# Writing the product of gate and value back into PSUM and splitting it from there, in a windowed attention with two gated MLPs

## The chip, the cores and the metric

The kernel runs on one core of a Trainium2 chip. The metric is the device time of one execution in microseconds, the median of several runs. The engines are named as in the profile: PE (TensorE matmuls) and PEld (its weight loads), DVE (VectorE), ACT (ScalarE), POOL (GpSimd) and SP (the queue that issues all DMAs). SBUF is the working memory of all engines; PSUM is the memory into which PE writes its products.

## The reference, cut to what matters

```python
scores = np.where(mask, scale * q @ k.T, -1e9)        # 4 x 8 heads, 576 positions, window 64
x = (softmax(scores) @ v)                             # -> 2304 tokens x 512
gate = 1.0 / (1.0 + np.exp(-(x @ w_gate)))            # 512 x 1536
x = (gate * (x @ w_val)) @ w_out                      # first MLP ("phase 0")
return ((x @ w_a) * (x @ w_b)) @ w_out2               # second MLP ("phase 1")
```

The six weight matrices come as 64-bit numbers and are decoded on the chip. Every matmul is done three times over, with both operands split into a high part of PE's reduced float format and the low rest (high by high, high by low, low by high).

## The kernel before, in words

The 2304 tokens stand in nine blocks of 256 columns. A slice of 128 of the 1536 hidden features is called F; each F has three weight tiles, `a` (gate), `b` (value) and `o` (out). For each slice the kernel makes a gate product and a value product on PE, multiplies the two, splits the result into high and low part, and later projects it with `o`.

The work runs through four stages. A **ramp** (0 to 75 us) has the attention and the first hidden slices in an order written out by hand. The **first MLP of the front blocks** (75 to 340 us) runs with the rest of the attention beside it. Then comes the **second MLP of the front blocks** (340 to about 612 us), while the weights of that MLP are still being decoded. Last come **the back blocks** (612 us to the end), whose weights are read back in split form. Outside the ramp and some runs of instructions that `in_order` ties, the order on each engine comes from the framework's scheduler, which has its own simulated times.

There are two ways in which gate times value is made.

- `hidden` calls `up` twice and then `gated`. `up` fills two PSUM tiles, `gps` (gate) and `vps` (value), of the pool `ps_gv`, which has three banks. `gated` moves the gate to SBUF as `hr` (ACT, a tanh in phase 0, a copy in phase 1), DVE multiplies `hr` with `vps` into `hr`, and `split_hidden` makes the two parts: ACT writes the high part `hh` from `hr`, then DVE writes the low part `hl` from `hr` and `hh`.
- `quad` takes two slices of tokens and features at once with seven products in place of eight (a Strassen-like scheme), in the order 1, 5, 6, 2, 7, 4, 3, each of six 512-column matmuls, into three banks `qa`, `qb`, `qc` of `ps_gv` and `ps_at` in turn, so that quad n+2 uses the pool of quad n. Between products ACT copies `qa` to SBUF (`keep_sum`: tiles `r`, line L845) and DVE adds `r` to a bank (`plus`, L848). `finish(0, ..)` and `finish(1, ..)` make the two results: gate `g[i]` times value (L853 in phase 0, L857 in phase 1) into `g[i]`, then the split as above, `hh`/`hl` for the first result and one tile `h` with both parts for the second.

In the quads of phase 0 but the last (`second is None`), the back blocks go on with seven products in the projection too: there `difference` (L900) reads `g[0]` and `g[1]` in SBUF, and the second result is not split.

A bank of a pool goes to the next tile in the program whose turn it is when its last reader in the program's order has come; the bank that is let go first is given out first.

The weight decode of one tile runs over three engines in a row: ACT `low` (L375) and `ex` (L378), DVE `wi` (L381, L384), POOL `wi` (L388), DVE `ex` (L394), ACT the high part (L400), DVE or POOL the low part (L403). For the quads POOL and ACT then make four sums of `a` and `b` (`s` L447, `wq` L449 and L450).

Of the kernel before, what the change touches and what calls it, by code (L numbers as in the profile page):

```python
# [14 lines left out]
AF = mybir.ActivationFunctionType  # L15
ALU = mybir.AluOpType
# [5 lines left out]
def tile_window_attention_gated_mlps(ctx, tc, q, k, v, w1g, w1v, w1o, w2a, w2b, w2o, out):  # L22
    nc = tc.nc
# [54 lines left out]
    for e in range(2):  # L78
        rows = slice(e * WIN, (e + 1) * WIN)
        nc.gpsimd.affine_select(  # L80
            out=mask_n[rows], in_=mask_n[rows], pattern=[[1, P]], compare_op=ALU.is_ge,
# [3 lines left out]
            out=mask_n[rows], in_=mask_n[rows], pattern=[[-1, P]], compare_op=ALU.is_ge,  # L85
# [175 lines left out]
    def quarter(i, j, nm):  # L261
        return xs.tile([P, 2, W], F32R, tag=f"q{i}{j}", name=f"{nm}{i}{j}")
# [32 lines left out]
    def whole(steps):  # L295
        while True:
            try:
                next(steps)
            except StopIteration as end:
                return end.value  # L300
# [172 lines left out]
    def split_hidden(phase, dst, hr):  # L473

        factor = 0.5 if phase == 0 else 1.0
        hh, hl = dst
        nc.scalar.activation(out=hh, in_=hr, func=AF.Copy, scale=factor)  # L477
        yield
        nc.vector.scalar_tensor_tensor(
            out=hl, in0=hr, scalar=factor, in1=hh.bitcast(F32), op0=ALU.mult, op1=ALU.subtract  # L480
        )
        yield dst

    def gated(phase, ps, n):
        hr = tmp.tile([P, W], F32, tag="hr", name="hr")[:, 0:n]
        if phase == 0:

            nc.scalar.activation(out=hr, in_=ps["a"], func=AF.Tanh, scale=0.5)
            yield
            nc.vector.scalar_tensor_tensor(out=hr, in0=hr, scalar=1.0, in1=ps["b"], op0=ALU.add, op1=ALU.mult)  # L490
        else:
            nc.scalar.activation(out=hr, in_=ps["a"], func=AF.Copy)
            yield
            nc.vector.tensor_tensor(out=hr, in0=ps["b"], in1=hr, op=ALU.mult)
        yield
        h = tuple(hp.tile([P, W], F32R, tag=f"h{p}", name=f"h{p}")[:, 0:n] for p in "hl")
        yield from split_hidden(phase, h, hr)

    def up(ps, nm, w, x):
        ps[nm] = ps_gv.tile([P, x[0].shape[-1]], F32, tag="gv", name="gps" if nm == "a" else "vps")  # L500
# [2 lines left out]
    def hidden(phase, w, x):  # L503
        ps = {}
        for nm in "ab":
            up(ps, nm, w, x)
        *_, h = gated(phase, ps, x[0].shape[-1])
        return h
# [312 lines left out]
    def multiply(ps, w, x, first):  # L821
        (wh, wl), (xh, xl) = w, x
        n = 0
        for c in range(2):
            for a, b in ((wh, xh), (wh, xl), (wl, xh)):
                nc.tensor.matmul(  # L826
                    ps, lhsT=a[:, c * P:(c + 1) * P], rhs=b[:, c, :], start=first and n == 0, stop=n == 5,
                    skip_group_check=True,
                )
                n += 1  # L830
# [3 lines left out]
    def products(ph, w, x, g, second):  # L834


        nquad[0] += 1
        bank, tag = (ps_gv, "gv") if nquad[0] % 2 else (ps_at, "at")
        pa, pb, pc = (bank.tile([P, W], F32, tag=tag, name=f"q{nm}") for nm in "abc")
        prod = lambda n, ps, first: multiply(ps, w[n], x[n], first)  # L840
        r, h = {}, []

        def keep_sum(ps, n):
            r[n] = late["rs"].tile([P, W], F32, tag="r", name=f"r{n}")
            nc.scalar.activation(out=r[n], in_=ps, func=AF.Copy)  # L845

        def plus(dst, ps, n):
            nc.vector.tensor_tensor(out=dst, in0=ps, in1=r[n], op=ALU.add)  # L848

        def finish(i, vv):  # L850
            if ph == 0:
                nc.scalar.activation(out=g[i], in_=g[i], func=AF.Tanh, scale=0.5)
                nc.vector.scalar_tensor_tensor(  # L853
                    out=g[i], in0=g[i], scalar=1.0, in1=vv, op0=ALU.add, op1=ALU.mult
                )
            else:
                nc.vector.tensor_tensor(out=g[i], in0=vv, in1=g[i], op=ALU.mult)  # L857
            if i == 0:
                t = tuple(hp.tile([P, W], F32R, tag=f"h{p}", name=f"h{p}") for p in "hl")
            elif second is None:  # L860
                h.append(None)
                return
            else:
                t = second()
                t = (t[:, 0], t[:, 1])
            whole(split_hidden(ph, t, g[i]))
            h.append(t)

        steps = {
            1: (lambda: prod(1, pa, True), lambda: keep_sum(pa, 1)),  # L870
            5: (lambda: prod(5, pb, True),),
            6: (lambda: prod(6, pa, False), lambda: keep_sum(pa, 2)),
            2: (lambda: prod(2, pc, True), lambda: plus(g[0], pc, 1)),
            7: (lambda: prod(7, pa, False), lambda: keep_sum(pa, 3), lambda: plus(r[3], pb, 3)),
            4: (lambda: prod(4, pa, False), lambda: finish(0, pa)),
            3: (lambda: prod(3, pb, False), lambda: plus(g[1], pb, 2)),
        }

        def step(n):
            for f in steps[n]:  # L880
                f()

        def end():
            finish(1, r[3])
            return tuple(h)

        return step, end

    def quad(ph, w, x, fill, g, second, between):
        step, end = products(ph, w, x, g, second)  # L890
        for i, n in enumerate((1, 5, 6, 2, 7, 4, 3)):
            step(n)
            fill(i)
        between()
        return end()
# [81 lines left out]
    def ramp_turns():  # L977
        waiting = []
        for n, (group, fcs) in enumerate(plan[:len(FIRST)]):
            hs = []  # L980
            for i, fc in enumerate(fcs):
                ps = {}

                def after(ps=ps, fc=fc, n=len(group) * N, hs=hs):
                    for h in gated(0, ps, n):
                        if h:
                            hs.append((parts[fc], h))
                        yield

                for nm in "ab":  # L990
                    matmuls.append(lambda ps=ps, nm=nm, fc=fc, group=group: up(ps, nm, parts[fc], x[0, group]))
                rest_of.append(after())
                for _ in range(-(-len(waiting) // (len(fcs) - i))):
                    job, number = waiting.pop(0)
                    for j in range(number):
                        cell = []

                        def mm(job=job, cell=cell):
                            m, a = next(job)
                            cell.append(a)  # L1000
                            m()

                        def ev(cell=cell):
                            cell[0]()
                            yield

                        matmuls.append(mm)
                        rest_of.append(ev())
# [104 lines left out]
    for fc in range(NF):  # L1113
# [16 lines left out]
        g = [tmp.tile([P, W], F32, tag="hr", name=f"g{i}") for i in range(2)]  # L1130
# [53 lines left out]
    for n, (ph, fc) in enumerate(steps):  # L1184
# [12 lines left out]
        if by_seven and fc % PAIR == 0:  # L1197
            g = quarter(0, 1, "g").bitcast(F32)
            g = [g[:, i] for i in range(2)]
            second = None  # L1200
        else:
            g = [tmp.tile([P, W], F32, tag="hr", name=f"g{i}") for i in range(2)]
            second = None if by_seven else (lambda a=((pairs_done - SEVEN) % 2, (fc + 1) % 2): quarter(*a, "h"))
# [4 lines left out]
        if ph and p == 0:  # L1208
            both.append((w["o"], *products(ph, w, x_ops, g, second)))
            if fc == 0:  # L1210
                continue
            since = len(nc.cur_bb.bb.instructions)
            for i, k in TOGETHER:
                both[i][1](k)
                if (i, k) == (0, 3):
                    hs.append((both[0][0], both[0][2]()))
            hs.append((w["o"], both[1][2]()))
            in_order(since, (mybir.EngineType.PE,))
        else:
            hs.append((w["o"], quad(ph, w, x_ops, slots(number, (ph, fc) == (0, PAIR)), g, second, between)))  # L1220
# [10 lines left out]
        if by_seven:  # L1231
            sums = []
            for i in range(2):
                t = late["sums"].tile([P, 2, 2, CH], F32R, tag="t", name=f"s{i}")
# [7 lines left out]
            b = {1: b11, 2: b21, 3: b22, 5: t1[0], 6: t2, 7: t3}  # L1242
# [59 lines left out]
```

## Time and profile before

| | us |
|---|---|
| median of 3 runs | 979.86 (979.34 to 980.27) |
| the profiled execution's own time | 978.29 |
| its span, first to last instruction | 976.3 |
| PE busy | 933.9 (96%) |
| DVE busy | 715.4 (73%) |
| ACT busy | 480.2 (49%) |
| POOL busy | 371.3 (38%) |

The span is what the views of the trace cover; the other 2 us of the profiled execution lie around it. An engine's busy time says how full it is, and what it waited for is read from the views of waits.

### The profile page before, as it was taken

The numbers are of one execution on the slowest core, as the hardware profiler recorded it, in microseconds if no ns is written. First come the engines' busy times: TensorE is split into PE (matmuls) and PEld (weight loads), VectorE is DVE, ScalarE is ACT, GpSimd is POOL, SyncE is SP. The second block draws the span as 40 slices with busy tenths as digits, with TensorE's granted clock in tenths as the row PEclk, the third lists the DMA queues.
The fourth block names the chain that finished last, engine by engine and source line by source line (L and its number), as shares of the span: only waits on it lengthen the run. The fifth ranks groups of instructions, "written<-read, shape, count | busy, mean of one in ns | idle before, by whom it ended". The sixth has DMA issues, their size and how long they took to land.

```text
span 976.3 us, 15657 instructions
## 1 busy us (share of the span) xinstructions
PE 933.9 (96%) x5504; PEld 775.3 (79%) x5504; DVE 715.4 (73%) x1339; ACT 480.2 (49%) x1053; POOL 371.3 (38%) x357
## 2 busy tenths in 40 slices
PE   7899999999999988989999997999999999999998
PEld 6798888887788876867777785787888888888886
DVE  6997877888754698888988976768888673444545
ACT  7896665576554455664545433563444233212111
POOL 4443233245522667785647736544440000000000
PEclk9999999999999998999999999999999999999999
DMA  9986699998852455665646567344456656554322
GB/s 221 256 217 195 245 325 323 301 309 269 260 189 87 158 177 181 228 232 200 237 162 217 210 207 244 112 153 141 151 171 217 227 191 208 161 165 114 121 65 87
DMA packets 146846, 193.70 MB, mean 198 GB/s; under 512 B 63824, under 2 KB 99152, under 8 KB 146768
## 3 DMA queue, kind: packets, MB, share of 16 engines
q1 hardware_dynamic: 146768, 192.71, 60.8%
q8 instruction: 43, 0.70, 0.3%
q14 instruction: 35, 0.29, 0.1%
HBM read 118.75 MB, written 69.47 MB: 193 GB/s over the span
## 4 chain that ended last, share of the span: by engine, by line
PE 64%; DVE 14%; POOL 10%; DMA 5%; issue 4%; ACT 2%; SPq 0%; POOLq 0%; DVEq 0%; ACTq 0%
PE qa L826 15%; PE accq L961 9%; PE qb L826 7%; PE vps L468 7%; PE gps L468 7%; PE accm L569 5%; POOL s L447 4%; PE qc L826 3%; POOL wi L388 3%; PE accy L924 3%; POOL wq L450 2%; PE accx L924 2%; DVE ex L394 2%; PE xps L228 2%; DVE wi L384 1%
## 5 line engine op out<-in xcount | busy, mean ns | idle before, releaser
L388 POOL TENSOR_TENSOR wi<-wi,low 128x512 int32<-128x512 int32 x72 | 105.8, 1469 | 137.2 <-DVE wi L384 102.9
L826 PE MATMUL qa<-op,wq 128*128 128x512 f32 x432 | 114.5, 395 | 5.7 <-ACT r L845 5.6
L826 PE MATMUL qb<-op,wq 128*128 128x512 f32 x432 | 112.2, 393 | 1.6 <-ACT op L730 0.8
L450 POOL TENSOR_TENSOR wq<-s,wq 128x256 fp32r<-128x256 f32 x96 | 90.2, 948 | 55.7 <-ACT wq L449 55.5
L845 ACT ACTIVATE r<-qa 128x512 f32<-128x512 f32 x108 | 62.0, 592 | 93.8 <-PE qa L826 78.6
L468 PE MATMUL gps<-xh,wa 128*128 128x256 f32 (+1 forms) x392 | 104.9, 336 | 0.6 <-DVE hr L490 0.6
L468 PE MATMUL vps<-xh,wb 128*128 128x256 f32 (+1 forms) x392 | 105.2, 338 | 0.0
L826 PEld LDWEIGHTS qa<-op,wq 128*128 128x128 f32 x432 | 81.7, 190 | 24.4 <-ACT r L845 7.4
L826 PEld LDWEIGHTS qb<-op,wq 128*128 128x128 f32 x432 | 81.8, 190 | 19.8 <-ACT op L730 1.0
L569 PE MATMUL accm<-hh,wo 128*128 128x512 f32 (+1 forms) x296 | 86.1, 360 | 2.8 <-DVE gacc L546 2.8
L468 PEld LDWEIGHTS gps<-xh,wa 128*128 128x128 f32 x392 | 69.2, 190 | 9.2 <-DVE hr L490 1.0
L961 PE MATMUL accq<-wo,h 128*128 128x512 f32 (+1 forms) x300 | 72.0, 383 | 4.7 <-DVE resf L965 3.1
L394 DVE SCALAR_TENSOR_TENSOR ex<-ex,wi 128x512 f32<-128x512 f32 x72 | 56.9, 790 | 25.0 <-POOL wi L388 16.2
L468 PEld LDWEIGHTS vps<-xh,wb 128*128 128x128 f32 x392 | 68.9, 190 | 7.9 <-DVE g L857 0.2
L961 PEld LDWEIGHTS accq<-wo,h 128*128 128x128 f32 x300 | 54.5, 188 | 17.7 <-DVE resf L965 4.4
L468 PE MATMUL gps<-xl,wa 128*128 128x256 f32 (+1 forms) x196 | 65.5, 334 | 0.6 <-DVE xl L237 0.6
L468 PE MATMUL vps<-xl,wb 128*128 128x256 f32 (+1 forms) x196 | 65.5, 334 | 0.0
L826 PE MATMUL qa<-op,wb 128*128 128x512 f32 x216 | 58.7, 408 | 6.0 <-ACT r L845 6.0
L477 ACT ACTIVATE hh<-g 128x512 fp32r<-128x512 f32 x36 | 22.7, 630 | 81.4 <-DVE g L857 50.8
L569 PEld LDWEIGHTS accm<-hh,wo 128*128 128x128 f32 x296 | 53.0, 191 | 11.1 <-ACT wq L449 3.2
L449 ACT ACTIVATE wq<-s 128x256 fp32r<-128x256 f32 x96 | 39.4, 414 | 41.0 <-POOL s L447 31.8
L189 ACT ACTIVATE pr<-pr,stat 128x128 f32<-128x128 f32 x144 | 54.1, 390 | 10.6 <-DVE stat L183 7.9
(173 smaller groups left out, 2152.0 us busy)
## 6 DMA issues: line engine op xcount, KB each, us to landing
wo<-ko SPq DMA_DIRECT2D x27, 512.0 KB, 4.0
wa<-ka SPq DMA_DIRECT2D x27, 512.0 KB, 4.3
st_o<-in_moe_w_out_dram SPq DMA_DIRECT2D x24, 512.0 KB, 4.7
ka<-wa SPq DMA_DIRECT2D x24, 512.0 KB, 5.0
kb<-wb SPq DMA_DIRECT2D x24, 512.0 KB, 3.9
ko<-wo SPq DMA_DIRECT2D x24, 512.0 KB, 4.2
kq<-wq SPq DMA_DIRECT2D x48, 256.0 KB, 3.3
wq<-kq SPq DMA_DIRECT2D x48, 256.0 KB, 3.1
```

The costliest lines, as they stand in the source:

```text
L189: nc.scalar.activation(out=pr[e][:, j, :], in_=pr[e][:, j, :], func=AF.Exp, bias=nmax[:, e, j:j + 1], scale=-1.0, accum_out=None if t in O ...
L388: nc.gpsimd.tensor_tensor(out=wi, in0=wi, in1=low, op=ALU.add)
L394: nc.vector.scalar_tensor_tensor(out=wf, in0=wf, scalar=SMALLEST, in1=wi.bitcast(F32), op0=ALU.is_ge, op1=ALU.mult)
L447: nc.gpsimd.tensor_tensor(out=s, in0=x, in1=y, op=op)
L449: nc.scalar.activation(out=t[:, 0], in_=s, func=AF.Copy)
L450: nc.gpsimd.tensor_tensor(out=t[:, 1], in0=s, in1=t[:, 0].bitcast(F32), op=ALU.subtract)
L468: nc.tensor.matmul(ps, lhsT=a[:, c * P:(c + 1) * P], rhs=b[:, c, :], start=(n == 0), stop=(n == 3 * NP - 1))
L569: nc.tensor.matmul(ps[:, m], lhsT=a[:, sl], rhs=b, start=k == 0, stop=k == total - 1)
L826: nc.tensor.matmul(ps, lhsT=a[:, c * P:(c + 1) * P], rhs=b[:, c, :], start=first and n == 0, stop=n == 5, skip_group_check=True,)
L845: nc.scalar.activation(out=r[n], in_=ps, func=AF.Copy)
L924: nc.tensor.matmul(bank[k], lhsT=a[n][i][:, sl], rhs=b[n][j], start=start and m == 0, stop=m == 2, skip_group_check=True,)
L961: nc.tensor.matmul(ps, lhsT=a, rhs=b, start=n == 0, stop=n == len(pairs) - 1)
```

## The change: what it does

In `gated` the product of gate and value is written over the value in its PSUM bank `vps` and no longer to `hr`; both parts are split from there. In `finish` the first result is written over `qa` and split from `qa`. The second result, where it is split, is written over `qc`: the seventh product's sum `plus(.., pb, 3)` now goes to the bank `qc` and not to the SBUF tile `r[3]`, and the product and the split read `qc`. Where `difference` later needs `g[0]` in SBUF, a new ACT copy (line 869 of the changed kernel) moves `qa` there after the split.

```diff
 def gated(phase, ps, n):
...
-            nc.vector.scalar_tensor_tensor(out=hr, in0=hr, scalar=1.0, in1=ps["b"], op0=ALU.add, op1=ALU.mult)
+            nc.vector.scalar_tensor_tensor(out=ps["b"], in0=hr, scalar=1.0, in1=ps["b"], op0=ALU.add, op1=ALU.mult)
...
-            nc.vector.tensor_tensor(out=hr, in0=ps["b"], in1=hr, op=ALU.mult)
+            nc.vector.tensor_tensor(out=ps["b"], in0=ps["b"], in1=hr, op=ALU.mult)
...
-        yield from split_hidden(phase, h, hr)
+        yield from split_hidden(phase, h, ps["b"])
...
         def finish(i, vv):
+            f = vv if i == 0 or second is not None else g[i]
             if ph == 0:
                 nc.scalar.activation(out=g[i], in_=g[i], func=AF.Tanh, scale=0.5)
                 nc.vector.scalar_tensor_tensor(
-                    out=g[i], in0=g[i], scalar=1.0, in1=vv, op0=ALU.add, op1=ALU.mult
+                    out=f, in0=g[i], scalar=1.0, in1=vv, op0=ALU.add, op1=ALU.mult
                 )
             else:
-                nc.vector.tensor_tensor(out=g[i], in0=vv, in1=g[i], op=ALU.mult)
+                nc.vector.tensor_tensor(out=f, in0=vv, in1=g[i], op=ALU.mult)
...
-            whole(split_hidden(ph, t, g[i]))
+            whole(split_hidden(ph, t, f))
+            if second is None:
+                nc.scalar.activation(out=g[i], in_=f, func=AF.Copy)
             h.append(t)
...
-            7: (lambda: prod(7, pa, False), lambda: keep_sum(pa, 3), lambda: plus(r[3], pb, 3)),
+            7: (lambda: prod(7, pa, False), lambda: keep_sum(pa, 3), lambda: plus(pc, pb, 3)),
...
-            finish(1, r[3])
+            finish(1, pc)
```

Since `qc` is now read until the end of its quad, the banks are handed on in another order: before, the next quad of the same pool got for its `qa` the bank of `qc`, which was let go after product 2; now it gets a bank that is let go only behind product 4 of that quad or later. The scheduler's order moves with it. On PE, in the second MLP of the front blocks, `qa_6298` is the first bank of the ninth quad, `qa_5966`, `qb_5967` that of the seventh, `qa_6164`, `qc_6166` of the eighth, and `accq` are projections. Before, the ninth quad's first product stood ahead of the seventh quad's products 7 and 4 (`wq7`, then `wb` into `qa_5966`):

```order
L826 MATMUL qc_6166<-op2_4628,wa_5852 128x512 x6
L826 MATMUL qa_6298<-op100_4624,wa_5986 128x512
L826 MATMUL qa_6298<-op101_4625,wa_5986 128x512
L826 MATMUL qa_6298<-op100_4624,wa_5986 128x512 x2
L826 MATMUL qa_6298<-op101_4625,wa_5986 128x512
L826 MATMUL qa_6298<-op100_4624,wa_5986 128x512
L826 MATMUL qa_5966<-op7_4764,wq7_5729 128x512 x6
```

In the changed kernel it stands behind the seventh quad's product 4, with 24 matmuls between:

```order
L826 MATMUL qa_5966<-op4_4769,wb_5697 128x512 x6
L826 MATMUL qa_6164<-op6_4762,wq6_5890 128x512 x4
L826 MATMUL qb_5967<-op3_4771,wq3_5734 128x512 x3
L964 MATMUL accq_6089<-wo_5368,h1_5827 128x512 x3
L964 MATMUL accq_6089<-wo_5518,h1_5961 128x512 x3
L826 MATMUL qb_5967<-op3_4771,wq3_5734 128x512
L964 MATMUL accq_6097<-wo_5368,h1_5827 128x512 x3
L964 MATMUL accq_6097<-wo_5518,h1_5961 128x512 x3
L826 MATMUL qb_5967<-op3_4771,wq3_5734 128x512 x2
L826 MATMUL qa_6164<-op6_4762,wq6_5890 128x512 x2
L826 MATMUL qa_6298<-op100_4624,wa_5986 128x512
```

What moved is the place of six matmuls: from ahead of two products of the quad before last to behind them. On ACT, in the back blocks of phase 0, the order around one new copy (L869) in the changed kernel is this; `qa_7138` is the bank of one quad and `qa_7232` that of the next, `r1` its `keep_sum`:

```order
L477 ACTIVATE hh_7187<-qa_7138 128x512
L449 ACTIVATE wq3_7227<-s3_7225 128x256
L853 ACTIVATE g01_7137<-g01_7137 128x512
L845 ACTIVATE r1_7241<-qa_7232 128x512
L869 ACTIVATE g01_7137<-qa_7138 128x512
L477 ACTIVATE t1_7293<-g01_7137 128x512
```

The copy is new there, and the tanh of the second gate (L853) and the next quad's first `keep_sum` stand ahead of it as they stood before.

## Rows read from the trace of the kernel before

**Rows 1.** Busy time by stage: us, then each engine's busy us (instructions), PEclk, DMA share, GB/s

```profile
0.00:75.00 75.00, 66.17 (x902) 58.13 (x903) 64.43 (x258) 62.65 (x199) 34.33 (x44) 1.00 0.90 233
75.00:340.00 265.00, 261.54 (x1850) 220.60 (x1849) 191.32 (x442) 154.93 (x377) 101.76 (x87) 1.00 0.74 242
340.00:612.00 272.00, 246.77 (x1146) 200.29 (x1145) 227.23 (x302) 140.12 (x259) 176.71 (x155) 0.97 0.60 208
612.00:976.30 364.30, 359.43 (x1612) 296.32 (x1610) 232.39 (x340) 122.47 (x221) 58.51 (x73) 1.00 0.47 153
```

**Rows 2.** PE's waits in 340 to 612 us: total us, times, longest

```profile
PE qa L826 <- ACT r L845: 10.9, 10, 2.7
PE accq L961 <- DVE resf L965: 4.7, 4, 2.0
...
PE accq L961 <- DVE hl L479: 1.2, 2, 0.9
```

**Rows 3.** DVE groups in 340 to 612 us: count, busy us, mean ns, idle before

```profile
L479 DVE SCALAR_TENSOR_TENSOR hl<-g,hh 128x512 fp32r<-128x512 f32 x12 | 12.7, 1061 | 3.8 <-ACT hh L477 3.6
L479 DVE SCALAR_TENSOR_TENSOR h<-g,h 128x512 fp32r<-128x512 f32 x12 | 11.7, 974 | 0.0
...
L857 DVE TENSOR_TENSOR g<-r,g 128x512 f32<-128x512 f32 x12 | 10.2, 848 | 0.0
L848 DVE TENSOR_TENSOR r<-qb,r 128x512 f32<-128x512 f32 x13 | 8.9, 686 | 7.1 <-ACT r L845 6.9
...
L857 DVE TENSOR_TENSOR g<-qa,g 128x512 f32<-128x512 f32 x12 | 8.2, 683 | 3.6 <-PE qa L826 3.6
...
L479 DVE SCALAR_TENSOR_TENSOR hl<-hr,hh 128x256 fp32r<-128x256 f32 x10 | 8.0, 803 | 3.5 <-ACT hh L477 3.5
...
L494 DVE TENSOR_TENSOR hr<-vps,hr 128x256 f32<-128x256 f32 x9 | 3.7, 414 | 0.0
```

**Rows 4.** Line L857 in the whole span: ns min/median/max

```profile
L857 DVE TENSOR_TENSOR g<-qa,g x24: 676/692/692, 379.9 to 960.0; 128x512 f32<-128x512 f32 x24
L857 DVE TENSOR_TENSOR g<-r,g x24: 677/682/1227, 385.1 to 962.6; 128x512 f32<-128x512 f32 x24
```

**Rows 5.** Timeline around one long split: start us, us, engine, instruction, idle before

```profile
481.81 1.61 POOL L388 TENSOR_TENSOR wi<-wi,low 128x512 int32<-128x512 int32 x1 [2.35 <-ACT hh L477]
482.18 1.78 DVE L479 SCALAR_TENSOR_TENSOR hl<-g,hh 128x512 fp32r<-128x512 f32 x1
...
484.02 0.73 PE L961 MATMUL accq<-wo,hl 128*128 128x512 f32 x2 [0.34 <-DVE hl L479]
```

**Rows 6.** Chain that ended last, 340 to 612 us: start us, us, what

```profile
382.81 1.15 DVE hl L479
...
482.27 1.70 DVE hl L479
...
548.08 1.10 DVE h L479
```

**Rows 7.** ACT groups in 340 to 612 us

```profile
L845 ACT ACTIVATE r<-qa 128x512 f32<-128x512 f32 x39 | 21.8, 585 | 4.0 <-DVE g L848 2.1 <-PE qa L826 1.9
L477 ACT ACTIVATE hh<-g 128x512 fp32r<-128x512 f32 x13 | 8.2, 627 | 11.6 <-DVE g L857 8.1 <-DVE g L853 3.4
```

**Rows 8.** DVE's largest split group in 0 to 340 us

```profile
L479 DVE SCALAR_TENSOR_TENSOR hl<-hr,hh 128x512 fp32r<-128x512 f32 x22 | 18.6, 843 | 7.4 <-ACT hh L477 7.2
```

**Rows 9.** PE's wait on a product in 0 to 340 us

```profile
PE gps L468 <- DVE hr L490: 0.6, 1, 0.6
```

**Rows 10.** Timeline, PE and DVE: ninth quad's first product, the next, seventh quad's split

```profile
486.11 1.52 PE L826 MATMUL qa<-op,wa 128*128 128x512 f32 x6
487.47 0.84 PE L826 MATMUL qa<-op,wq 128*128 128x512 f32 x3
...
497.97 0.69 DVE L479 SCALAR_TENSOR_TENSOR hl<-g,hh 128x512 fp32r<-128x512 f32 x1 [0.70 <-ACT hh L477]
```

**Rows 11.** POOL's waits in 340 to 612 us

```profile
POOL wi L388 <- DVE wi L384: 29.4, 9, 9.5
POOL s L447 <- DMA wf<-kf: 21.3, 3, 15.3
```

## The prediction

> **What bounds the kernel now.** I begin with the busy time by stage [rows 1]. From 75 to 340 us PE is busy 261.54 of 265 us, and from 612 us to the end 359.43 of 364.3: there it has almost nothing to win, whatever the other engines do. The ramp is busy 66.17 of 75, and the change's lines have little to do in it. Only from 340 to 612 us does PE stand idle for long, 272 − 246.77 = 25.2 us, and there DVE is busy 227.23 us, or 84%. Its granted clock is 0.97 on the mean there, against 1.00 elsewhere, so in a few short stretches PE ran at the lower of its two levels. That too comes back if the idle time goes.
>
> PE's waits in that stage [rows 2] are led by the first products of quads and the products after them, which wait for ACT's copy to free a bank (10.9 us in 10 waits). Projections wait for DVE's residual (4.7) and for the low part (1.2). ACT's copies themselves stand behind DVE (the copies in [rows 7] name it ahead of 2.1 of their 4.0 us), and DVE's additions behind those copies (6.9 us in [rows 3]). This is a chain of three engines in a fixed order, which DVE's length sets in part.
>
> The groups of DVE there [rows 3] show what stretches. Operations that read two SBUF tiles take 1061 ns (`hl<-g,hh`), 974 (`h<-g,h`), 848 (`g<-r,g`), and 803 at half width. Of the same shape, those with one operand in PSUM take 683 and 686 (414 at half width). The whole span's extremes [rows 4] say that it is not their plain cost: `g<-qa,g` lies between 676 and 692, and `g<-r,g` has the same minimum, 677, and nearly the same median, 682, but goes up to 1227. What runs beside them is seen at one place [rows 5]: a split of 1.78 us with POOL's 1.61 us of work beginning 0.37 us ahead of it, and then a projection that waited 0.34 us for it. So I read it as contention of two SBUF readers, from which an operand in PSUM frees DVE.
>
> **The change: DVE's relief.** After it, the split of either result reads one operand in PSUM, and so does the second result's product. In 340 to 612 us that is, from [rows 3], 12 × (1061 − 683) = 4.5 us, 12 × (974 − 683) = 3.5, 12 × (848 − 683) = 2.0, and 10 × (803 − 414) = 3.9: together 13.9 us of DVE's time. That is the upper end of what the stage can gain. The lower end is 0, if DVE's ends are never what comes last. Between them I take what lies on the chain that ended last. It holds eight such pieces from 340 to 612 us, the first, longest and last of them in [rows 6]: 1.15, 1.31, 1.21, 0.99 (a half-width one), 1.18, 1.70, 1.14 and 1.10 us. Over 0.69 (0.41 for the half one) that is 0.46 + 0.62 + 0.52 + 0.58 + 0.49 + 1.01 + 0.45 + 0.41 = 4.5 us. **I take −4.5.**
>
> In 0 to 340 us the splits of hidden slices have 22 × (843 − 683) = 3.5 us of the same kind [rows 8]. PE is busy beside nearly all of it, since of its 3.5 idle us from 75 to 340 one wait of 0.6 on a product stands behind this sort of work [rows 9]. **I take −0.5**, between 0 and 3.5. The same wait is where the change can cost: `vps` is now held until the split is done, some 0.63 + 0.69 us longer by [rows 3, 7], and if it comes late, the next slice's `gps` waits. With three banks and PE ahead of DVE, this should happen at a few places at most. I price it at 0 here and keep 1.3 us for each place.
>
> **Writes into PSUM by DVE.** No row of before has one. The bounds are 683 ns (one PSUM operand, SBUF result) and 1061 (the contended sort). They are like the first in that one side only is in SBUF, so I take 683. The extra that the upper bound would give is priced as a rival. ACT's high part is read from PSUM now: 585 in place of 627 ns [rows 7], a gain too small to count.
>
> [...]
>
> **New copies on ACT.** Ten copies of `qa` back to SBUF, about 0.585 us each [rows 7], are 5.9 us in the back blocks, where ACT is busy 122.47 of 364.3 us [rows 1]. The changed order puts each behind the next tanh and the next quad's first `keep_sum`, so nothing that PE soon needs is behind it but a high part. PE's 359.43 busy us hide them, and I count 0. Without that cover it is up to 0.6 each, 5.9 at the most.
>
> **Banks.** A quad's `qc` is held to its end now, so the quad after next begins in a bank that is free only behind product 4. Before, the ninth quad's first product began at 486.11 us, and the seventh quad's first result was split at 497.97 + 0.69 = 498.66 [rows 10]: 12.5 us too early for the new rule, so it has to move, as the order shows. Of ten quads in this stage I read such an early start in five (third, seventh to tenth). If PE has other matmuls in its place, it costs nothing. In the changed order 24 stand between product 4 and the moved product. One takes (487.47 − 486.11)/6 = 0.227 us [rows 10], so they are 5.4 us. What must happen meanwhile is the product, 0.68, the high part, 0.63 or less, and the low part, 0.69 (rows as above): 2.0 us plus short waits. Covered, so 0; uncovered, a whole product of 1.36 us each, 5 × 1.36 = 6.8.
>
> **The sum.** −4.5 − 0.5 = −5.0 us against the profiled execution's own 978.29 is 973.3. That execution was 1.57 us below the median of the runs, 979.86, so for the median I forecast **974.9 us**.
>
> **The rivals.** No change within 0.2% of before, 2 us (about what a measurement of this kernel can tell): the 340-to-612 us stage is paced by the weights' decode and not by DVE. For it speaks that POOL is busy 176.71 us there [rows 1], that its sums wait 21.3 us for the weights' DMA, and its decode 29.4 us for DVE's `wi` [rows 11], an operation that the change leaves alone. Then the relief turns into idle time of DVE, and the time is 979.9. Against it: PE's own waits name no weight tile among the large ones [rows 2].
>
> Slower, by uncovered handovers: the moved products leave PE nothing ready, because the projections that stand in their place wait too, for DVE's residual as before (4.7 us in [rows 2]). Five of them are 6.8 us, against relief of which only half arrives, 2.3 us, as DVE's gain comes after the wait: 979.86 + 6.8 − 2.3 = 984.4 with the front's −0.5 left out; with the whole 4.5 it is 982.2. I name 982.2 for it. It decides from the fourth of the five uncovered on (4 × 1.36 = 5.4 against 5.0). Against it stands the count of 24 matmuls.
>
> Slower, by dear writes: about 46 operations in the stage now write PSUM (9 half-width and 24 full-width products, 13 additions). At the upper bound each costs 1061 − 683 = 0.38 us more, some 17 us of DVE against 13.9 relieved. Scaled as the relief was (4.5 of 13.9 on the chain) it is +5.6 − 4.5 = 1.1, about 981; if more of it lands on the path, 983. No row speaks for it; that no row excludes it is all.
>
> **How the numbers follow.** The forecast has 0.60. Its own range goes from 967.5 (974.9 less 7.4, about half of the 13.9 that could come and the clock's lower stretches with it) to 977.8 (the edge of what counts as faster). No change: 0.16. Uncovered handovers: 0.17. Dear writes: 0.07, of which a little would still end within 2 us of before, which the forecast's own tail on the fast side balances. The range that holds 8 in 10 needs all but the worst of the slow cases, 967.5 to 983. Faster by over 0.2%: 0.61; within: 0.16; slower: 0.23.
>
> **What would show it.** Each step right: from 340 to 612 us the splits have a mean near 0.69 us and none over 0.75; the products written into `vps`, `qa` and `qc` take 0.68 (0.41 at half width); DVE's busy time there falls by about 14 us and PE's idle time from 25 to about 20; the last stage stays at 364.3 us with ten copies of 0.59 on ACT. Wrong: splits that are still long would mean that POOL isn't what stretches them; PE waits on `qa` behind DVE's `hl` or `h` would be the handovers; waits on `gps` behind `hl` below 340 us the longer hold of `vps`; products over 0.8 us the dear writes; and DVE's relief with PE as idle as before, the decode.

## The result: faster by 11.6 us

The changed kernel takes 968.02 us (966.23 to 971.76 in four runs) against 979.6 for the kernel before beside it: a ratio of 0.9889, with a 95% interval of 0.9853 to 0.9925. The forecast was 974.9 us with a range of 967.5 to 983.0. The sign is right and the time lies just inside the fast end; the gain is more than twice the 5.0 us that the sum gave. The profiled execution took 969.65 us, with a span of 967.5; that of the kernel before took 978.29, so the rows below compare two executions that are 8.6 us apart.

The busy time by stage, in the columns of [rows 1], says where it came from:

```profile
0.00:75.00 75.00, 65.75 (x890) 57.77 (x892) 63.85 (x255) 62.55 (x198) 33.99 (x43) 1.00 0.91 234
75.00:340.00 265.00, 258.67 (x1841) 217.69 (x1836) 181.15 (x440) 150.21 (x370) 94.97 (x84) 0.99 0.72 235
340.00:612.00 272.00, 256.63 (x1205) 211.00 (x1204) 218.20 (x312) 147.88 (x274) 177.32 (x164) 0.98 0.63 216
612.00:967.50 355.50, 350.64 (x1578) 290.11 (x1578) 223.89 (x334) 121.51 (x222) 54.13 (x68) 1.00 0.47 156
```

From 340 to 612 us PE does 1205 matmuls in place of 1146, and its idle time falls from 25.2 us to 272 − 256.63 = 15.4. DVE is busy 218.20 us in place of 227.23, with 312 instructions in place of 302; it fell by 9.0 us and not by the 14 of the forecast, with ten more instructions in the same window. The front gains nothing: from 75 to 340 us PE is busy 2.9 us less than before. The last stage gains nothing either: PE is idle for 4.9 us of it in both kernels, and its window is shorter because it begins at a fixed 612 us.

PE's waits from 340 to 612 us have changed places (total us, times, longest):

```profile
PE accq L964 <- ACT hh L477: 5.6, 4, 3.1
PE qa L826 <- ACT r L845: 2.3, 3, 1.1
PE accm L569 <- DVE gacc L546: 1.9, 2, 1.0
PE accq L964 <- DVE resf L968: 1.7, 2, 1.3
...
PE accq L964 <- DVE hl L479: 0.5, 1, 0.5
...
PE gps L468 <- DVE hl L479: 0.2, 1, 0.2
```

The wait that led in [rows 2], products behind ACT's copies, is down from 10.9 us to 2.3. Projections now wait longer for high parts (1.4 before, 5.6 now). A product that begins late behind a split, which the handover rival had foretold, shows once, with 0.2 us.

The groups of DVE in that stage answer to [rows 3] (count, busy us, mean ns, idle before):

```profile
L848 DVE TENSOR_TENSOR qc<-qb,r 128x512 f32<-128x512 f32 x13 | 9.0, 692 | 3.8 <-ACT r L845 3.7
L479 DVE SCALAR_TENSOR_TENSOR hl<-qa,hh 128x512 fp32r<-128x512 f32 x13 | 8.9, 687 | 5.5 <-ACT hh L477 5.3
...
L858 DVE TENSOR_TENSOR qc<-qc,g 128x512 f32<-128x512 f32 x12 | 8.3, 689 | 0.1
L858 DVE TENSOR_TENSOR qa<-qa,g 128x512 f32<-128x512 f32 x12 | 8.3, 688 | 2.0 <-PE qa L826 2.0
L479 DVE SCALAR_TENSOR_TENSOR h<-qc,h 128x512 fp32r<-128x512 f32 x12 | 8.2, 683 | 3.1 <-ACT h L477 2.9
...
L479 DVE SCALAR_TENSOR_TENSOR hl<-vps,hh 128x256 fp32r<-128x256 f32 x10 | 4.2, 417 | 3.6 <-ACT hh L477 3.6
```

Every length is as forecast: 687, 683, 689 and 417 ns stand where 1061, 974, 848 and 803 stood, and writing into PSUM costs 5 to 6 ns (692 and 688 against 686 and 683).

### The profile page after: what moved, and what is told of

Same layout as the page of the kernel before. It is cut to its first block, busy times and chain, and to the rows that moved or that the text cites. A ratio compares the mean times of both kernels' runs of the same rounds, so it can differ in the third digit from the quotient of the medians.

```text
span 967.5 us, 15682 instructions
## 1 busy us (share of the span) xinstructions
PE 931.7 (96%) x5504; PEld 776.6 (80%) x5504; DVE 687.1 (71%) x1339; ACT 482.1 (50%) x1063; POOL 360.4 (37%) x357
## 4 chain that ended last, share of the span: by engine, by line
PE 68%; POOL 10%; DVE 9%; DMA 6%; issue 3%; ACT 3%; POOLq 0%; SPq 0%; DVEq 0%; ACTq 0%
PE qa L826 15%; PE accq L964 12%; PE qb L826 8%; PE gps L468 7%; PE vps L468 7%; PE accm L569 5%; PE qc L826 4%; POOL s L447 3%; POOL wi L388 3%; PE accy L927 3%; POOL wq L450 2%; PE accx L927 2%; DMA kf<-ex 2%; PE xps L228 2%; DMA wf<-kf 1%
## 5 line engine op out<-in xcount | busy, mean ns | idle before, releaser
L388 POOL TENSOR_TENSOR wi<-wi,low 128x512 int32<-128x512 int32 x72 | 101.8, 1413 | 136.3 <-DVE wi L384 99.3
L477 ACT ACTIVATE hh<-qa 128x512 fp32r<-128x512 f32 x36 | 21.5, 598 | 90.1 <-DVE qa L858 61.2
L964 PE MATMUL accq<-wo,hh 128*128 128x512 f32 x184 | 56.3, 397 | 5.8 <-ACT hh L477 5.6
L189 ACT ACTIVATE pr<-pr,stat 128x128 f32<-128x128 f32 x144 | 54.1, 391 | 12.3 <-DVE stat L183 11.9
L210 POOL TENSOR_TENSOR pr<-pr,stat 128x512 f32<-128x512 f32 x34 | 38.1, 1122 | 55.0 <-DVE stat L208 36.7
```

The source lines that it names most:

```text
L189: nc.scalar.activation(out=pr[e][:, j, :], in_=pr[e][:, j, :], func=AF.Exp, bias=nmax[:, e, j:j + 1], scale=-1.0, accum_out=None if t in O ...
L210: (nc.vector if t in OTHERS["norm"] else nc.gpsimd).tensor_tensor(out=pr[e], in0=pr[e], in1=den[:, e].unsqueeze(2).to_broadcast([P, NP, P] ...
L388: nc.gpsimd.tensor_tensor(out=wi, in0=wi, in1=low, op=ALU.add)
L964: nc.tensor.matmul(ps, lhsT=a, rhs=b, start=n == 0, stop=n == len(pairs) - 1)
```

## The experiments

**The contention by itself.** A kernel without attention and MLPs runs DVE's split operation 16 times in a row in each of seven stretches; in four of them GpSimd adds two SBUF tiles beside it. `x`, `y`, `z` are in SBUF, `u`, `w` in PSUM.

```diff
+    pool()                     # 8 x gpsimd.tensor_tensor(out=po, in0=pa, in1=pb), all in SBUF
+    for _ in range(16):
+        stt(z, x, y)           # then stt(z, u, y), stt(w, u, y), stt(w, x, y)
```

> No attention and no MLP: only DVE's operation of the split, 128x512, 16 times in a row in each of seven stretches, and GpSimd additions of two SBUF tiles beside it in four of them. Contention theory: alone, two SBUF operands and one in PSUM take the same, 0.68 to 0.70 us, whether the result goes to SBUF or PSUM; beside GpSimd the operation with two SBUF operands takes 1.0 or more into either memory, and the ones with an operand in PSUM stay at 0.68 to 0.70. If a write into SBUF counts as well, the form with the result in SBUF takes longer than that with the result in PSUM. Rival: the long splits came from DMA or ACT, and GpSimd changes nothing.

Groups by stretch (count, busy us, mean ns): first alone (`z<-x,y`, `z<-u,y`, and GpSimd, there with a multiplication), then beside GpSimd, each with GpSimd's own group, an addition.

```profile
L29 DVE SCALAR_TENSOR_TENSOR z<-x,y 128x512 f32<-128x512 f32 x16 | 11.1, 692 | 0.5
...
L29 DVE SCALAR_TENSOR_TENSOR z<-u,y 128x512 f32<-128x512 f32 x16 | 11.0, 691 | 0.5
...
L54 POOL TENSOR_TENSOR po<-pa,pb 128x512 f32<-128x512 f32 x7 | 8.8, 1262 | 0.5
...
L29 DVE SCALAR_TENSOR_TENSOR z<-x,y 128x512 f32<-128x512 f32 x16 | 18.6, 1162 | 0.5
L40 POOL TENSOR_TENSOR po<-pa,pb 128x512 f32<-128x512 f32 x8 | 12.7, 1586 | 1.5 <-DVE pa L36 0.9
...
L29 DVE SCALAR_TENSOR_TENSOR w<-x,y 128x512 f32<-128x512 f32 x16 | 18.6, 1165 | 0.5
...
L29 DVE SCALAR_TENSOR_TENSOR z<-u,y 128x512 f32<-128x512 f32 x16 | 11.1, 691 | 0.5
L40 POOL TENSOR_TENSOR po<-pa,pb 128x512 f32<-128x512 f32 x8 | 10.1, 1267 | 7.6 <-DVE pa L36 7.1
```

Alone, two SBUF operands take 692 ns and one in PSUM 691. Beside GpSimd the first takes 1162 on the mean, whichever memory it writes (1165 into PSUM), and the second stays at 691. The mean mixes two lengths, since GpSimd is busy for only 12.7 us of the stretch; the shortest, the median and the longest of the 16 (ns) show it:

```profile
L29 DVE SCALAR_TENSOR_TENSOR z<-x,y x16: 680/1162/1635, 54.4 to 72.8; 128x512 f32<-128x512 f32 x16
```

So what stretches this operation is the reading of two SBUF tiles while GpSimd works on SBUF tiles, 1162 ns against 691. Both engines pay: GpSimd's addition takes 1586 ns there, and 1267 beside the operation with one operand in PSUM.

**The two halves of the change.** One kernel (`e1_gated`) changes only `gated`, as in the diff; the other (`e2_quads`) is the changed kernel without these lines.

```diff
...
-            nc.vector.tensor_tensor(out=hr, in0=ps["b"], in1=hr, op=ALU.mult)
+            nc.vector.tensor_tensor(out=ps["b"], in0=ps["b"], in1=hr, op=ALU.mult)
...
-        yield from split_hidden(phase, h, hr)
+        yield from split_hidden(phase, h, ps["b"])
```

> Only the hidden slices of one F (the function gated) have their product in PSUM; the quads are as before. Relief theory (every us that DVE is relieved of in 340 to 612 us comes out of the time there, since DVE is on PE's path): the half-width splits there fall from 803 to about 415 ns, 10 of them, so PE gains about 4 us between 340 and 612 us. Handover theory (the gain came from the quads' banks, which are held and handed on differently): nothing in that stage. In the front, the changed kernel was 5.7 us later than before by the time PE had done 300 us of matmuls; if the longer hold of vps does that, this kernel loses some 5 us there too, and its time is 976 to 981; if the front's loss has another source, 975 by the relief theory and 979.6 by the other.

> Only the quads are changed, both results and the bank of the seventh product's sum; the hidden slices of one F are as before. Relief theory: 10 of the 13.9 us of DVE's relief in 340 to 612 us are here, so some 10 us less, 969 to 970. Handover theory: the whole of it, 966 to 969. If the front's loss of 5.7 us belongs to vps, it is gone here and PE's first 300 us of matmuls end as in before.

Before took 980.27 us beside them. `gated` alone takes 976.35 (0.9947, 0.992 to 0.9974); the quads alone 968.38 (0.9857, 0.983 to 0.9885), which can't be told from the whole change. The two gains, 3.9 and 11.9 us, would make 15.8; together they make 11.6.

The front shows a cost of `gated`. The first row is PE's wait from 75 to 340 us with `gated` alone; the changed kernel has the second:

```profile
PE vps L468 <- ACT hr L488: 2.7, 1, 2.7
```

```profile
PE vps L468 <- ACT hr L488: 3.3, 1, 3.3
```

Neither the kernel before nor the quads alone has it; four more kernels with `gated` changed and an order made for it have it with 2.5 to 3.5 us. As I read it, the bank that `vps` held up to its split is the one missing: at 265.19 us in the changed kernel, `vps` must take the one that a gate's tanh lets go, and the tanh stood behind an `ex` that ACT could begin only at 264.19 us, after a wait of 1.60 us for DVE. This does not explain the 4 us that are missing from the sum of the two gains, because `gated` alone has nearly the same wait and is 3.9 us faster all the same. Why they do not add up stays open.

How far a single profile can be trusted in the front is seen from the kernels whose orders on PE, DVE and ACT are those of before up to the first quads. In them the same instruction begins at other times; the last columns are its first and last start, in the kernel before, with the quads alone, and in the two kernels below (second result over `qb`; bank alone):

```profile
L730 ACT ACTIVATE op<-gacc x7: 1045/1057/1063, 329.0 to 371.9; 128x1024 fp32r<-128x1024 f32 x7
```

```profile
L730 ACT ACTIVATE op<-gacc x7: 1042/1057/1064, 334.3 to 377.8; 128x1024 fp32r<-128x1024 f32 x7
```

```profile
L730 ACT ACTIVATE op<-gacc x7: 1041/1057/1063, 332.9 to 375.9; 128x1024 fp32r<-128x1024 f32 x7
```

```profile
L730 ACT ACTIVATE op<-gacc x7: 1043/1057/1067, 332.1 to 375.6; 128x1024 fp32r<-128x1024 f32 x7
```

The front's end moves by 5 us from execution to execution of one and the same order. So a difference of that size there says nothing in one profile, and the comparisons below go by medians.

**The bank and the operands, apart.** Three kernels change only quads. One (`e3_qb`, the first line of the diff) writes the first result over `qa`, as the changed kernel does, and the second over `qb`, and leaves `qc` as it was; one (`e4_hold`, the next four) puts the seventh product's sum into `qc`, from where the product reads it, but splits both results from SBUF; one (`e5_holdonly`, the rest) only holds `qc` to the end, with one DVE addition of a single column.

```diff
+            f = pa if i == 0 else pb if second is not None else g[1]
...
-            7: (..., lambda: plus(r[3], pb, 3)),
+            7: (..., lambda: plus(pc, pb, 3)),
...
-            finish(1, r[3])
+            finish(1, pc)
...
             finish(1, r[3])
+            late = g[1] if second is None else h[1][1].bitcast(F32)
+            nc.vector.tensor_tensor(out=pc[:, 0:1], in0=pc[:, 0:1], in1=late[:, 0:1], op=ALU.add)
```

> Quads alone; the second result is written over qb in place of qc and the seventh product's sum stays in SBUF, so that qc is let go after product 2 as in before. Relief theory: the two splits fall to 0.69 us, 12 x 0.37 + 12 x 0.29 = 8 us of DVE's relief, and the second result's product stays at 0.85; the time is 971 to 972. Handover theory: without the new handover of qc no more than 2 us are gained, 978 to 980.

> The bank alone: the seventh product's sum goes to qc and the second result's product reads it there, but both results and the hidden slices are written to SBUF and split from there as in before. Relief theory: only the second result's product is relieved, 12 x 0.165 = 2 us, so 977.5 to 978.5. Handover theory: the products that begin later on PE give nearly the whole gain, 967 to 971. The rival of the prediction by which the later handover costs: 981 or more.

> The kernel before, with no operand moved to PSUM; a DVE addition of one column reads and writes qc behind the second result's split, so that qc is held to the end of its quad and the banks are handed on as in the changed kernel. [...] Handover theory: the bank alone gained 5.7 us in the run with the seventh sum in qc, 2 of which are the relief of the second result's product, so some 3.7 us less than before, 976 to 977. Relief theory (nothing but DVE's shorter operations gains): 980 to 981. The prediction's rival of uncovered handovers: over 982.

Over `qb`: 973.61 us (0.9906, 0.9873 to 0.9939). Sum in `qc`: 974.57 (0.9931, 0.9911 to 0.9952). Hold alone: 982.51 (1.0026, 1.0012 to 1.004). The twelve additions of one column took 156 ns each in 340 to 612 us, 1.9 us together. So holding the bank with them gains nothing by itself, it costs some 2.5 us, and the handover theory falls as it was put; relief without the new handover gains 6.7. The kernel with the sum in `qc` gained more than the 2 us that its one relieved product could bring by [rows 3], and why is not settled: its order is another one too.

**Both reliefs, `qc` as before.** The kernel `e3b_qb_gated` has the lines of `e1_gated` and of `e3_qb` together:

> The second result over qb, as in the run e3_qb, and the hidden slices of one F as in the changed kernel: nearly the changed kernel's relief (the second result's product alone stays on two SBUF tiles, 2 us), and the banks handed on as before. If the parts add up: 6.7 + 3.9 = 10.6 us less than before, 969 to 970. If the hidden slices add nothing beside relieved quads, as the change with and without them (968.0 and 968.4) has it: 973 to 974, and the handover is then what the changed kernel has more.

It takes 976.38 (0.9963, 0.9946 to 0.998), slower than the result over `qb` without `gated`. Neither expectation had this: relief was added, and time was lost. What differs besides is the order that the scheduler made.

**The order held fast.** For the next kernels every engine's order was written into the kernel as a list and tied by dependencies without a semaphore. In the traces of the two kernels that follow here, the operations of each engine stand in the order that was to be kept. The kernel before with these ties and no other change was not run, so what they cost by themselves is not shown; from 612 to 964 us PE is idle for 1.61 us with them (`x1_border_relief`) and for 1.45 in the kernel before. The code is shortened:

```python
for k in order:                       # one engine's instructions by their place in the program
    i = program[k]
    if last is not None:
        tc.add_manual_dep(i, last, NoSync, reason="replay")
    last = i.name
```

The first (`x1_border_relief`) has the order of before and the operands of `e3b_qb_gated`, but for the quads of phase 0 that `difference` follows:

> The order of every engine is that of the kernel before, instruction for instruction, written out as dependencies that cost nothing on the chip. Only operands differ: the first result over qa, the second over qb, the hidden slices over vps, as in the run e3b_qb_gated (the last slice's quads of phase 0 without the projection's sums as before). DVE is relieved of 11.9 us in 340 to 612 us by the rows of before. If each us counts: 968. If a third counts, as the prediction took it: 976. If the gain is that of the new order alone: 980, and the 976.4 of e3b_qb_gated was its order's.

It takes 981.72 against 981.0 (1.0005, 0.999 to 1.002): the relief earns nothing in that order. DVE was relieved, its busy time from 340 to 612 us is 213.13 us in place of 227.23, but PE waits elsewhere and is idle for 23.9 us against 25.2. The stage, in the columns of [rows 1], and PE's waits in it:

```profile
340.00:612.00 272.00, 248.07 (x1148) 201.99 (x1147) 213.13 (x301) 139.34 (x259) 167.06 (x155) 0.97 0.62 209
```

```profile
PE qc L826 <- DVE h L479: 6.7, 5, 2.7
PE qa L826 <- ACT r L845: 4.9, 5, 2.5
PE qb L826 <- DVE hl L479: 2.8, 3, 1.7
PE qc L826 <- DVE hl L479: 2.0, 1, 2.0
PE vps L468 <- DVE hl L479: 1.9, 3, 0.9
...
PE vps L468 <- DVE h L479: 1.0, 1, 1.0
```

Products behind splits, which hold banks that products once let go: 6.7 + 2.8 + 2.0 + 1.9 + 1.0 = 14.4 us. That is the handover rival, uncovered. PE's other idle time has fallen from 25.2 us to 23.9 − 14.4 = 9.5, and these waits have taken its place. How much of that fall is the relief's is not separated, since an engine that PE waits for later gains time while PE stands at a bank. In the changed kernel, whose order was made for the held banks, 0.2 us of it are left.

The second (`x2_aorder_dose`) has the changed kernel's order and operands, with an extra DVE addition behind each split of the second MLP, of which the scheduler knew nothing. In a kernel run before it (`e6_dose`) the scheduler knew of the additions, which stood behind the quads' splits alone:

```diff
             whole(split_hidden(ph, t, f))
+            if second is not None:
+                m = 230 if i == 0 else 144
+                nc.vector.tensor_tensor(out=f[:, 0:m], in0=f[:, 0:m], in1=t[1][:, 0:m].bitcast(F32), op=ALU.add)
```

> The changed kernel with DVE's relief given back in the quads that split both results: behind the first result's split an addition of 230 columns on qa, some 0.39 us, behind the second's one of 144 on qc, some 0.30, both with an operand in PSUM; 12 of each in 340 to 612 us, 8.2 us in all. The output is not the reference's order of work (a dead bank is written once more). If each us of DVE counts there, as the profiles of before and after read, the time rises by 8, to 976; if a third of it lies on the chain, as the prediction took it, by 2.6, to 970.6; if the handover made the gain, it stays at 968.

> The order of every engine is that of the changed kernel, and its operands too; behind each split of the second MLP stands one more DVE addition of 256 columns on the split's own PSUM bank, 0.41 us each, which the scheduler did not know of when it made the order. From 340 to 612 us these are 34, 14.1 us, about what the change relieved DVE of (13.9). A dead bank is written once more; the output is the same. If each us of DVE counts: 982. If a third: 972.6. If the order made the gain, or the scheduler's knowledge of the lengths doesn't matter: 968 to 969.6, as the run e6_dose.

With 8.4 us that the scheduler knew of (12 additions of 395 ns and 12 of 306 in that stage): 969.57 (0.9883, 0.986 to 0.9906), the changed kernel's own time. With additions that it did not know of: 977.79 (0.9966, 0.9948 to 0.9984). The stage from 340 to 612 us in the columns of [rows 1], of the first and of the second:

```profile
340.00:612.00 272.00, 255.77 (x1209) 209.93 (x1208) 225.67 (x338) 147.51 (x274) 174.88 (x167) 0.99 0.64 217
```

```profile
340.00:612.00 272.00, 248.95 (x1171) 202.39 (x1169) 228.80 (x339) 141.45 (x264) 171.02 (x159) 0.99 0.63 213
```

In both, DVE is about as busy as in the kernel before (227.23 us); PE is idle for 16.2 us in the first, nearly as short as in the changed kernel, and for 23.1 in the second. The additions in the second are, by the groups of that stage,

```profile
L484 DVE TENSOR_TENSOR qc<-qc,h 128x256 f32<-128x256 f32 x12 | 5.2, 433 | 0.4
L484 DVE TENSOR_TENSOR qa<-qa,hl 128x256 f32<-128x256 f32 x12 | 5.2, 432 | 0.4
...
L484 DVE TENSOR_TENSOR vps<-vps,hl 128x256 f32<-128x256 f32 x9 | 3.9, 433 | 0.3
```

14.3 us, and they cost 977.79 − 968.02 = 9.8 us by the medians, or (0.9966 − 0.9889) × 980 = 7.5 by the ratios, each beside its own runs of before. (The 27 additions outside the stage leave PE's idle time in the back blocks at 5.3 us against 4.9.) So in this order a us of added DVE time costs 0.5 to 0.7 us, and the intervals of the two ratios leave 0.25 to 0.8. Part of that is not DVE's time but banks, since the additions hold theirs longer; 3.0 us of PE's waits stand behind them:

```profile
PE qc L829 <- DVE qc L484: 1.9, 2, 1.4
...
PE gps L468 <- DVE qa L484: 1.1, 2, 0.6
```

Where the order was made anew, the 8.4 us cost nothing that the runs can tell: the intervals exclude that each us counts, but not that a third does.

**Orders made with other lengths.** If what costs is time that the scheduler doesn't reckon with, then an order made with longer splits should help the kernel before, and one made with longer decode operations the changed one. In both, DVE copies were put behind those operations when the order was made, and taken out again, so that the two kernels have the operations of the kernel before and of the changed one and differ from them in order alone.

> The kernel before with all its operands, contended as they are. Its order was made by the scheduler with one more DVE copy of 256 columns behind each split of the second MLP, and the copies were taken out again, so that the order reckons with splits that are some 0.3 to 0.4 us longer; every engine keeps that order. If contention costs because the order doesn't reckon with it, part of the change's gain comes without moving an operand: 970 to 976. If what counts is the splits' length itself, nothing: 979 to 982.

> The changed kernel with all its operands, in an order that the scheduler made with additional DVE copies (taken out again) behind the three operations of the second MLP's weight decode that are still long in its profile: ex 0.88 in place of 0.68, wi 0.92 to 1.02, and the low parts 0.91 to 1.02 us. If reckoning with contention helps, faster than the changed kernel, 960 to 966; if not, 967 to 971.

The kernel before in such an order takes 985.18 (1.0044, 1.0027 to 1.0061), slower than in its own and outside both of the times expected. The changed kernel takes 960.27 (0.979, 0.9767 to 0.9814), which beats both kernels: 7.8 us less than the changed one by the medians. Its stage from 340 to 612 us, in the columns of [rows 1]:

```profile
340.00:612.00 272.00, 259.88 (x1238) 215.18 (x1237) 220.41 (x319) 152.28 (x285) 177.86 (x171) 0.99 0.65 219
```

PE's idle time is 12.1 us, and 1238 matmuls are done in place of 1205. The second time came out as the theory had it and the first did not, so the theory that reckoning with contention is what helps is not shown.

## Why the prediction was right in sign and too small

**What bounds the kernel** was read rightly: the gain is in the stage from 340 to 612 us, where PE's idle time falls by 9.9 us, and the back blocks and the front gave none. In that stage the mean of the granted clock went from 0.97 to 0.98. Read in windows of 1 us, it stands at 1.00 or at 0.50, with values between only where it changes. In the kernel before it is at 0.50 from 347 to 350, 375 to 381 and 607 to 613 us, and each time the fall lies within 2 us of the end of one of PE's three longest idle stretches of the stage (2.8, 2.7 and 2.5 us). In the changed kernel it is at 0.50 from 354 to 357, 440 to 442 and 511 to 514 us, within 2 us of idle time of 1.9 (in four gaps), 3.1 and 1.9 us. How much of the gain is the clock's is not separated. The rival by which the decode paces that stage and nothing changes is out with it.

**Contention** held in every length, and the kernel of seven stretches shows it by itself.

**The relief's share on the path** is the term that came out too small, and how much of the difference is the relief's is not settled. Of 13.9 us the prediction took 4.5, the pieces on the chain that ended last, a share of 0.32. In the changed kernel's own order, added DVE time costs 0.5 to 0.7 a us, which would be 7 to 10 us for the 13.9; but the longer held banks are in it, and its interval, 0.25 to 0.8, has the 0.32 in it too. Three runs speak against a share that belongs to the relief alone. In the order of before the relief earns nothing. In the changed kernel's order, with DVE as busy as before, 3.3 us of the gain are left (0.9966 of before). In an order made with the additions in view (`e6_dose`) none of it is lost that the runs can tell, with DVE nearly as busy as before. So, as far as these runs show, the term that the prediction did not have is the new order itself: it counted a moved product as a cost that has to be covered, and had nothing for what a new order gains.

The chain's eight pieces may also be too narrow a reading, which is argued and not shown: the chain names the engine released last, and where PE waited for ACT's copies (10.9 us in [rows 2]) ACT had itself stood behind DVE for a part ([rows 7]). These waits fell to 2.3 us in the changed kernel, but the quads alone, which are as fast, keep most of them:

```profile
PE qa L826 <- ACT r L845: 7.2, 5, 2.2
```

**Handovers** at 0 were right for the changed kernel, by its wait of 0.2 us, and for the reason given: other matmuls stand in the moved products' place. That it is the order that covers them is borne out by the order of before with held banks, 14.4 us of waits and no gain; but an order made anew does not always do it, since the kernel that only holds `qc` (`e5_holdonly`) has 3.1 us of products waiting for that bank. The rival's price, 6.8 us, was too low for that kernel, where `qb` and `vps` are held longer besides `qa`. In that kernel the second result lies over `qb`, so it is not the changed kernel's handover to the letter.

**The front**, put at −0.5 us, went the other way: one wait of 3.3 us, as I read it the longer hold of `vps` that the prediction had named and kept 1.3 us a place for. What the front lost as a whole can't be told from single profiles, whose fronts differ by 5 us.

**Dear writes** fell (688 to 692 ns). ACT's high part from `qa`, for which the prediction had 585 ns, takes 597 in the stage from 340 to 612 us. **ACT's copies** cost nothing that can be seen: from 612 us on PE is busy 350.64 of 355.5 us with nine of the ten there, of 595 ns each, and is idle for 4.9 us as before.

```profile
L869 ACT ACTIVATE g<-qa 128x512 f32<-128x512 f32 x9 | 5.4, 595 | 0.1
```

**What stays open** is how much of the 11.6 us is the scheduler's luck. Every edit here gave another order. One with more relief came out slower (976.38 against 973.61), one with 8.4 us of relief given back came out as fast (969.57), and other orders for the same operands moved the time by +5 us (985.18 against 980.05) and −7.8 us. Which property of an order does it is not settled.

## What to carry to other kernels

When a DVE operation with two SBUF operands shows a spread of lengths beside GpSimd, leave one operand in PSUM: here it then took what it takes alone (691 ns against 692), and GpSimd's addition 1267 ns in place of 1586. The price is a bank that is held longer, so the order has to be made again around it; nearly the same operands in the old order gained nothing. Where a scheduler makes the order, its own effect can be nearly as large as the edit's (7.8 us beside 11.6 here), and it is found by holding the order fast and changing the operands alone.

## What the hardware showed beside that

GpSimd is slowed as well by DVE's two SBUF operands, from 1267 to 1586 ns for an addition of 128x512, and DVE's operation is as long whether it writes PSUM or SBUF (1165 against 1162 ns). The length of the front, 329.0 to 334.3 us up to its last operands' first instruction, varies by 5 us between executions of the same order.
